# GpSimd copies of VectorE score tiles: one tile an instruction in place of two

## The chip, the cores and the metric

The kernel runs on one core of one Trainium2 chip. The metric is the device time of one launch in microseconds (us); for repeated runs it is the median. Besides these times there is one profiled execution, with a trace of every instruction, and it has a time of its own.

## The reference, cut to what matters

Two independent pieces are computed and set side by side in the output, (1, 2048, 1280) in bf16. Piece A is a state-space layer, of sequence 2048 and width 640. Piece B is an attention with 32 query heads of 20 dimensions that share one key head and one value head:

```python
q = (x @ wq).reshape(B, S, 32, 20).transpose(0, 2, 1, 3)
k, v = x @ wk, x @ wv
scores = jnp.einsum("bhqd,bkd->bhqk", q, k) * 20 ** -0.5
o = jnp.einsum("bhqk,bkd->bhqd", softmax(scores), v)
b = o.transpose(0, 2, 1, 3).reshape(B, S, 640) @ wo
a = 2 * (scan_over_time(x_A @ B_bar) @ C).real + x_A * D     # h = Lam_bar * h + Bu
return concatenate([a, b], -1)
```

Piece B needs 2048 x 2048 x 32 exponentials, which are most of the work of this kernel that is not a matmul.

## The kernel before, in words

**Tiles.** The scores are made in 2048 tiles of 128 keys by 512 queries of one head (`NTILE`, L403). Sixty-four tiles make a block: 16 groups of keys for 4 heads. There are 32 blocks, and the product of probabilities and values (PV) of one block is gathered in one PSUM bank (`pvbank`). A block's bank is evacuated (L1470) when all its tiles have been multiplied in, and then the next block's PV starts.

**Two ways to an exponential.** ScalarE (ACT) takes two or three score tiles in one `Exp` instruction (L1139) and writes bf16 probabilities to `PR`. Some tiles take the other way, called D tiles here. For a D tile VectorE (DVE) reads the scores from PSUM and writes them as 16-bit integers whose bits, read as bf16, are a coarse exponential (`fill_d`, L1316, instruction at L1329). Three copies follow, each with a constant added to the integers (`SHIFTS`, L419), and PV takes the tile and its three copies with differently scaled values (`VS`), so that a D tile has four buffers of `DR` and four PV matmuls. `DR` has 18 buffers (`NDS`). Through helpers, the trace shows the first step as `DR<-SC` or `DR<-MB` at L603, a copy by DVE as `DR<-DR` at L603, and a copy by GpSimd (POOL) as `DR<-DR,step` at L598.

**Who copies.** The list `d_open` holds the D tiles that still need copies, oldest first, each with the numbers of the shifts left (1, 2, 3 at first). Two functions make copies from it. `copy_source` (L1348) is DVE's: it copies two tiles in one instruction where it can, otherwise one. It acts when nine or more copies are outstanding (`BACKLOG`), or when the current block has all its tiles and only waits for them, and then with the high priority `CLOSE`. `pool_source` (L1378) is POOL's: it takes the oldest tile's next shift and the first two tiles that still need that shift; with fewer than two it returns nothing. Both call `copy` (L1392), which takes free buffers, builds the access patterns and enters the results for PV. POOL works on pairs of 16-bit values as 32-bit integers, and its addend `step` repeats the constant in both halves.

**The order of the work.** Nothing is ordered by the chip at run time. A planner (`Schedule`, L40) plays the program on five engines with a duration for each step, always picking the ready step of lowest priority number, and the order in which it started the steps on each engine is emitted as the program, with semaphore waits where one engine needs another's result (`Emitter`, L246). So a planned duration decides where steps stand, while the real one decides when they run. The planner's numbers near the change are 663 ns for a D tile's first step, 342 and 210 ns for a DVE copy of two and of one tile, and 1040 ns for a POOL copy of two (`POOL2`).

**The port.** Steps marked `port=True` share one resource between DVE and POOL in the plan (L134 to L139, L176 to L182): neither engine starts such a step while the other has one under way, DVE may not follow for another 60 ns after POOL's (`LOCK`), and POOL does not start one while DVE has a better one held back (`port_wanted`). POOL's emitted step also waits for DVE's last port step before it (`op.after`). The copies of both engines are port steps, and so are many steps of piece A on DVE: the products `u`, the scans `g`, the products of `g` with the tables, `W` and a few small ones.

**How many D tiles.** A D tile is started by `fill` (L1105), in place of the third tile of an ACT instruction or beside it, or alone by `d_source` (L1285). All of them ask for at least four free `DR` buffers, for piece A not to be behind its due times (`behind`, L1199), and for the share of D tiles to be below 0.25. Near the end of a block, `can_d` (L1261) asks for more buffers before it starts on the next block. Every tile that doesn't become a D tile goes to ACT.

Of the kernel before, what the change touches and what calls it, by code (L numbers as in the profile page):

```python
# [14 lines left out]
I32 = mybir.dt.int32  # L15
# [394 lines left out]
class Build:  # L410
# [967 lines left out]
    def pool_source(self):  # L1378

        s = self.s  # L1380
        can = [d for d in self.d_open if d[1].end is not None and s.seen(d[1], "pool") <= s.t]
        if not can or len(self.d_free()) < 2:
            return None
        k = can[0][2][0]
        two = [d for d in can if k in d[2]][:2]
        if len(two) < 2 or self.short(two):
            return None
        return Op("pool", [], self.POOL2, prio=1, port=True, hook=lambda op: self.copy(op, k, two, True))

    POOL2 = 1040.0  # L1390

    def copy(self, op, k, tiles, pool=False):  # L1392
        p = self
        src = [d[0].index for d in tiles]
        free = self.d_free()[:len(tiles)]
        dst = [h.index for h in free]

        def at(x):
            if len(x) == 1:
                return p.DR[:, x[0], :]  # L1400
            return bass.AP(tensor=p.DR, offset=512 * x[0], ap=[[512 * p.NDS, 128], [512 * (x[1] - x[0]), 2], [1, 512]])
        if pool:
            def words(x):
                return bass.AP(tensor=p.DR, offset=512 * x[0], ap=[[512 * p.NDS, 128], [512 * (x[1] - x[0]), 2], [1, 512]]).bitcast(I32)
            add = bass.AP(tensor=p.step, offset=k, ap=[[4, 128], [0, 2], [0, 256]])
            op.fns.append(self.tt(words(dst), words(src), add, ALU.add))
            op.reads.append("step")
        else:
            op.fns.append(self.ts(at(dst), at(src), float(self.SHIFTS[k][0]), 0.0, ALU.add, ALU.max))
        op.reads += [f"DR{i}" for i in src]  # L1410
        op.writes += [f"DR{i}" for i in dst]
        for d, h in zip(tiles, free):
            h.taken, h.left, h.users = True, 1, []
            d[0].left -= 1
            d[0].users.append(op)
            d[2].remove(k)
            _, _, _, b, kc, j = d
            self.d_left[b, j] -= 1
            self.pv_entry(b, kc, j, k, h, op)
        self.d_open = [d for d in self.d_open if d[2]]  # L1420
# [619 lines left out]
```

## Time and profile before

| what | us |
|---|---|
| median of 4 runs | 765.25 |
| the 4 runs | 764.29 to 766.17 |
| the profiled execution's own time | 769.72 |
| its span, first to last instruction | 767.9 |
| busy in the span: ACT | 739.5 |
| busy in the span: PE (matmuls) | 702.0 |
| busy in the span: DVE | 680.5 |
| busy in the span: POOL | 431.2 |

Counted in the trace: 461 D tiles (397 from the bank group `SC`, 64 from the bank `MB`), 402 POOL copies of two tiles each, 263 DVE copies of two tiles and 53 of one, and 667 `Exp` instructions. That is 402 x 2 + 263 x 2 + 53 = 1383 copies, three for each D tile, and 2048 - 461 = 1587 tiles for ACT (414 instructions of two, 253 of three).

A row of a profile group reads: line, engine, operation, what it writes and reads, how often, then busy us and mean ns of one, then the idle time of the engine just before it and what ended it. The span of an instruction overlaps its successor's by some tens of ns where they run back to back, so that count times mean is a little above the busy time.

### The profile page before, as it was taken

Reading aid. Unit: us, or ns where it says so; the run is one execution under the profiler, and the core shown is the slowest. Engines: PE = TensorE matmul, PEld = TensorE weight load, DVE = VectorE, ACT = ScalarE, POOL = GpSimd, SP = SyncE. Lnnn points to the kernel's source line nnn. Section 1 sums busy time; section 2 is a strip of 40 time slices with the busy share of each in tenths; the row PEclk is TensorE's granted clock in tenths of the full one; section 3 lists DMA queues with packets and bytes.
Section 4 is the critical chain, followed back from the end, with each engine's and each line's share of the span. In section 5 each row is a group of like instructions: output and inputs, shape, how many; then the busy total and the mean of one; then the engine's idle time right before and its main releaser. Section 6 shows DMA issues by size and latency. Waiting matters only on the chain.

```text
span 767.9 us, 24175 instructions
## 1 busy us (share of the span) xinstructions
PE 702.0 (91%) x10231; PEld 233.1 (30%) x10231; DVE 680.5 (89%) x1282; ACT 739.5 (96%) x693; POOL 431.2 (56%) x450
## 2 busy tenths in 40 slices
PE   9998898888899999998999999989999999989986
PEld 3322222222233223222332323223222232333323
DVE  6787899899999998999999898889999999987795
ACT  5799999999999999999999999999999999999994
POOL 3657655246756356744656657447664545557560
PEclk9699999999999999999999999999999999999999
DMA  9734121000000111110000111130000010000101
GB/s 195 116 96 81 43 59 50 18 8 11 8 17 26 30 35 32 49 46 18 16 15 10 37 32 39 32 68 17 11 14 12 18 31 21 24 11 25 31 6 43
DMA packets 61770, 27.87 MB, mean 36 GB/s; under 512 B 44936, under 2 KB 61664, under 8 KB 61664
## 3 DMA queue, kind: packets, MB, share of 16 engines
q1 hardware_dynamic: 60332, 26.20, 14.7%
q8 instruction: 81, 1.33, 0.7%
q10 hardware_dynamic: 1332, 0.13, 0.2%
q14 instruction: 25, 0.20, 0.1%
HBM read 8.31 MB, written 8.12 MB: 21 GB/s over the span
## 4 chain that ended last, share of the span: by engine, by line
ACT 78%; PE 17%; DMA 2%; DVE 1%; issue 1%; POOL 0%; ACTq 0%; SPq 0%; POOLq 0%; DVEq 0%
ACT PR L1139 77%; PE SC L588 5%; PE MB L584 5%; PE MB L588 5%; PE SC L584 1%; DMA wqf<-in_B_wq_dram 1%; DMA qd<-QP 1%; DMA xaT<-in_A_x_dram 0%; DVE DR L603 0%; ACT tab L1707 0%; ACT PR L1625 0%; POOL fr L603 0%; DVE fr L603 0%; DVE mab L818 0%; DVE prod L598 0%
## 5 line engine op out<-in xcount | busy, mean ns | idle before, releaser
L1139 ACT ACTIVATE PR<-SC 128x1024 bf16<-128x1024 f32 (+1 forms) x667 | 723.2, 1295 | 10.5 <-PE SC L588 8.3
L598 POOL TENSOR_TENSOR DR<-DR,step 128x512 int32<-128x512 int32 x402 | 410.3, 1046 | 306.1 <-DVE DR L603 124.6
L588 PE MATMUL SC<-QT,KT 32*128 32x512 bf16 x1984 | 262.6, 386 | 50.5 <-ACT PR L1139 42.4
L603 DVE TENSOR_SCALAR DR<-SC 128x512 int16<-128x512 f32 x397 | 265.1, 684 | 36.4 <-PE SC L588 25.8
L588 PE MATMUL MB<-DR,VS 128*32 128x512 bf16 x1844 | 231.8, 386 | 0.6 <-DVE pvsb L1470 0.3
L588 PE MATMUL MB<-PR,VP 128*32 128x512 bf16 x1587 | 213.7, 385 | 3.0 <-POOL DR L598 1.3
L588 PEld LDWEIGHTS SC<-QT,KT 32*128 32x128 bf16 x1984 | 67.8, 91 | 289.8 <-ACT PR L1139 194.3
L603 DVE TENSOR_SCALAR DR<-DR 128x1024 int16<-128x1024 int16 (+1 forms) x316 | 115.0, 418 | 12.5 <-PE MB L588 9.5
L588 PEld LDWEIGHTS MB<-DR,VS 128*32 128x32 bf16 x1844 | 57.9, 94 | 65.3 <-issue 36.5
L588 PEld LDWEIGHTS MB<-PR,VP 128*32 128x32 bf16 x1587 | 54.2, 94 | 62.6 <-issue 39.6
L584 PE MATMUL MB<-xaT,BT 128*32 128x512 bf16 x800 | 57.8, 382 | 1.9 <-DMA xaT<-in_A_x_dram 1.3
L598 DVE TENSOR_TENSOR prod<-MB,Z 128x1024 bf16<-128x1024 f32 x40 | 48.6, 1214 | 4.2 <-PE MB L584 3.8
L603 DVE TENSOR_SCALAR DR<-MB 128x512 int16<-128x512 f32 x64 | 43.5, 680 | 2.5 <-PE MB L588 2.3
L588 PE MATMUL MB<-KT,VZ 128*32 128x256 bf16 x840 | 45.0, 274 | 0.0
L1810 DVE TENSOR_TENSOR_SCAN g<-sc,hst,u 128x512 bf16<-128x512 f32 x30 | 41.2, 1373 | 0.0
L598 DVE TENSOR_TENSOR prod<-g,tab 128x1024 bf16<-128x1024 bf16 x40 | 34.1, 852 | 0.0
L584 PE MATMUL MB<-CT,xbT 128*32 128x512 bf16 (+1 forms) x640 | 29.7, 301 | 0.2 <-issue 0.2
L584 PE MATMUL MB<-CT,W 128*32 128x512 bf16 (+1 forms) x640 | 29.1, 301 | 0.8 <-DVE prod L598 0.5
L1627 DVE CAST stg<-MB 128x512 bf16<-128x512 f32 x35 | 23.8, 680 | 5.3 <-PE MB L584 5.2
L584 PE MATMUL MB<-WO,OP 128*32 128x128 bf16 (+1 forms) x560 | 25.5, 290 | 0.0
L584 PE MATMUL MB<-xbT,wqf 128*32 128x512 bf16 x340 | 25.2, 396 | 0.0
L588 PEld LDWEIGHTS MB<-KT,VZ 128*32 128x32 bf16 x840 | 21.3, 96 | 12.5 <-issue 5.9
(140 smaller groups left out, 370.7 us busy)
## 6 DMA issues: line engine op xcount, KB each, us to landing
out_dram<-stg SPq DMA_DIRECT2D x35, 128.0 KB, 1.9
qd<-QP SPq DMA_DIRECT2D x20, 128.0 KB, 1.8
QT<-qd SPq DMA_DIRECT2D x28, 80.0 KB
OP<-pvsb SPq DMA_DIRECT2D x108, 20.0 KB
rdP<-recs SPq DMA_DIRECT2D x108, 20.0 KB
CT<-in_B_x_dram SPq DMA_DIRECT2D x2, 640.0 KB, 5.6
WO<-in_B_wo_dram SPq DMA_DIRECT2D x1, 800.0 KB, 4.6
wqf<-in_B_wq_dram SPq DMA_DIRECT2D x1, 700.0 KB, 6.0
```

What stands on the lines that cost most here:

```text
L584: r = e.matmul(out[32 * j:32 * j + 32], lhsT=lhsT[:, 32 * j:32 * j + 32], rhs=rhs, start=start, stop=stop, tile_position=(0, 32 * j), skip ...
L588: return lambda e: e.matmul(out, lhsT=lhsT, rhs=rhs, start=start, stop=stop, **kw)
L598: return lambda e: e.tensor_tensor(out, a, b, op)
L603: return lambda e: e.tensor_scalar(out, a, s1, s2, op0=op0, op1=op1)
L1139: ex = self.act(lambda e: e.activation(dst, t[:, 0:512 * n], ACT.Exp, scale=1.0 / UNIT), 0.8333 * 512 * n + 64, table="exp", deps=[op], re ...
L1627: ev = self.dve(lambda e: e.tensor_copy(st, bank.ap), 620, deps=[prev], reads=[bank.key], writes=[key], prio=self.EV, gate=(lambda: last.e ...
L1810: o = self.dve(lambda e, ri=ri, init=init: e.tensor_tensor_scan(p.g[:, u, ri, :], rdec, p.u[:, ri, :], init, ALU.mult, ALU.add), 1280, por ...
```

## The change

POOL's copy takes one tile in place of two. `pool_source` keeps its first test (some tile open, two buffers free), takes the oldest tile alone, doesn't return empty-handed when there is no second one, and plans 600 ns for the step in place of 1040. The access patterns in `copy` get a length of one. DVE's copies and all the rules for D tiles are as before.

```diff
@@ pool_source
         if not can or len(self.d_free()) < 2:
             return None
         k = can[0][2][0]
-        two = [d for d in can if k in d[2]][:2]
-        if len(two) < 2 or self.short(two):
-            return None
-        return Op("pool", [], self.POOL2, prio=1, port=True, hook=lambda op: self.copy(op, k, two, True))
-
-    POOL2 = 1040.0
+        two = [d for d in can if k in d[2]][:1]
+        return Op("pool", [], 600.0, prio=1, port=True, hook=lambda op: self.copy(op, k, two, True))
+
@@ copy
         if pool:
             def words(x):
-                return bass.AP(tensor=p.DR, offset=512 * x[0], ap=[[512 * p.NDS, 128], [512 * (x[1] - x[0]), 2], [1, 512]]).bitcast(I32)
-            add = bass.AP(tensor=p.step, offset=k, ap=[[4, 128], [0, 2], [0, 256]])
+                return bass.AP(tensor=p.DR, offset=512 * x[0], ap=[[512 * p.NDS, 128], [512 * (x[-1] - x[0]), len(x)], [1, 512]]).bitcast(I32)
+            add = bass.AP(tensor=p.step, offset=k, ap=[[4, 128], [0, len(src)], [0, 256]])
```

## The prediction

> **What bounds the kernel now.** I read the busy shares first, then the chain that ended last, then the groups of instructions.
>
> ```profile
> PE 702.0 (91%) x10231; PEld 233.1 (30%) x10231; DVE 680.5 (89%) x1282; ACT 739.5 (96%) x693; POOL 431.2 (56%) x450
> ...
> ACT 78%; PE 17%; DMA 2%; DVE 1%; issue 1%; POOL 0%; ACTq 0%; SPq 0%; POOLq 0%; DVEq 0%
> ...
> L1139 ACT ACTIVATE PR<-SC 128x1024 bf16<-128x1024 f32 (+1 forms) x667 | 723.2, 1295 | 10.5 <-PE SC L588 8.3
> L598 POOL TENSOR_TENSOR DR<-DR,step 128x512 int32<-128x512 int32 x402 | 410.3, 1046 | 306.1 <-DVE DR L603 124.6
> ```
>
> The reader is to see that ACT's exponentials (L1139) fill the span, with 10.5 us of idle time before them, and that they hold most of the chain. POOL has no share of the chain. So the time is how many tiles ACT must take, and POOL bears on it only through the number of D tiles: ACT spends 723.2 / 1587 = 0.456 us on a tile, so each D tile more or less is worth 0.456 us. What limits the D tiles? The stages view (busy time of each engine in the part in which D tiles are made, from 40 to 748 us) shows how full the others are:
>
> ```profile
> core 0: us, PE busy (x) PEld busy (x) DVE busy (x) ACT busy (x) POOL busy (x), PEclk, DMA share, GB/s
> ...
> 40.00:748.00 708.00, 651.43 (x9428) 212.34 (x9428) 641.27 (x1160) 703.20 (x650) 408.18 (x400) 1.00 0.12 30
> ```
>
> DVE has 708.0 - 641.3 = 66.7 us free, and the view of its waits gives most of that to waits for a score matmul, the longest of which are about 1 to 2 us. POOL has 300 us free, but the waits of its copies say why it can't use them:
>
> ```profile
> POOL DR L598 <- DVE DR L603: 124.6, 33, 10.9
> POOL DR L598 <- DVE g L1810: 61.3, 16, 12.1
> POOL DR L598 <- PE MB L588: 37.1, 35, 6.5
> POOL DR L598 <- DVE u L598: 23.7, 6, 11.2
> ```
>
> They end with DVE steps, most of them port steps. I laid the starts and ends of POOL's instructions and of DVE's port steps (copies, u, g, prod from g, W and xbT, OP, the small ones) side by side, and counted outstanding copies at each moment as three for each first step ended less the copies started. Of 704 us from 44 to 748, POOL holds the port for 406, DVE alone for 210, and neither for 88. Of these 88 us, 25 have no copy outstanding and 28 have exactly three: one fresh tile, no second one to make a pair. So the port is 88% full, and nearly all the rest belongs to no copy that could be made, or to the rule of two. A block's change shows it (timeline of POOL, then of DVE):
>
> ```profile
> 394.46 1.04 POOL L598 TENSOR_TENSOR DR<-DR,step 128x512 int32<-128x512 int32 x1 [4.09 <-PE MB L588]
> 400.33 5.02 POOL L598 TENSOR_TENSOR DR<-DR,step 128x512 int32<-128x512 int32 x5 [4.83 <-PE MB L588]
> ```
>
> ```profile
> 395.41 2.31 DVE L603 TENSOR_SCALAR DR<-DR 128x1024 int16<-128x1024 int16 x7 [0.51 <-PE MB L588]
> 397.63 0.68 DVE L603 TENSOR_SCALAR DR<-SC 128x512 int16<-128x512 f32 x1
> 398.23 1.28 DVE L1810 TENSOR_TENSOR_SCAN g<-sc,hst,u 128x512 bf16<-128x512 f32 x1
> 399.42 0.67 DVE L603 TENSOR_SCALAR DR<-SC 128x512 int16<-128x512 f32 x1
> ```
>
> DVE clears the old block's copies, makes a first step at 397.6, scans, makes a second one at 399.4, and only after that POOL starts, at 400.3.
>
> **What the Trainium skill says.** The page "SBUF — State Buffer", section "Who interferes with whom", says that DVE and GpSimd share one pair of ports as an exclusive lock held for the whole instruction, against DVE steps in two-port modes or with two SBUF inputs. The trace agrees: a DVE copy has a median of 418 ns and a longest of 1258, as if it had stood behind a POOL copy. "Perfetto Trace Analysis", section "GPSIMD Engine Instruction", says to time GpSimd by start-to-start spacing rather than by the reported span; here five copies in a row took 5.02 us, 1.00 us each, against a reported 1.037, so the difference is small. "GPSIMD Engine Reference", section 3.1, gives 4497 ns for a tensor_tensor of 2048 fp32, which is 2.2 ns an element; by it I estimate 562 ns for 256 elements. The trace's pair, 1.00 us for 512, is 1.96 ns an element.
>
> **The change part by part.** *Price of a single.* The trace has no copy of one tile. From below: half a pair, 0.50 us, if an instruction had no fixed cost; nothing suggests a smaller one. From above: GpSimd's memsets took 204 ns for 128 columns and 101 ns for one, so some 0.1 us is fixed there, and its tensor_scalar VS of only 80 columns took 448 ns; with a fixed 0.4 us in the pair, a single is (1.00 - 0.4) / 2 + 0.4 = 0.70. I take 0.59, between the estimate above plus a little and the planner's 600 ns, which sets the order in any case.
>
> *What it adds on the port.* POOL makes 800 copies in this part: 800 x 0.59 = 472 us against 408, so 64 more. *What it removes.* POOL no longer waits for a second tile: 28 us of the port become usable. The sum is 36 us too much for the port, and DVE must take copies over from POOL. The forms of DVE's copies:
>
> ```profile
> L603 DVE TENSOR_SCALAR DR<-DR 128x1024 int16<-128x1024 int16 x263 | 104.0, 444 | 12.4 <-PE MB L588 9.5 <-POOL DR L598 2.1
> ...
> L603 DVE TENSOR_SCALAR DR<-DR 128x512 int16<-128x512 int16 x53 | 12.9, 286 | 0.1
> ```
>
> In pairs a copy costs DVE 0.444 / 2 = 0.222 us, so each copy that moves frees 0.59 - 0.22 = 0.37 us of the port: 36 / 0.37 = 97 copies move, and DVE has 97 x 0.222 = 21.5 us more. DVE's pairs aren't broken up, since the shifts are taken in order: what the oldest tile still needs, the next one needs too.
>
> *What follows for ACT.* If DVE were full, the 21.5 us would come out of D tiles. One D tile less frees 0.67 us of DVE (265.1 / 397) and three copies, 1.77 us of the port, which brings 1.77 / 0.37 = 4.8 copies back to POOL, 1.06 us of DVE: 1.73 us in all, so 21.5 / 1.73 = 12.4 tiles, or 5.7 us of ACT. DVE has 66.7 us free in short pieces, so a part is hidden; I put 70% on the path, since those pieces are times in which it has no tile to work on. That is 9 tiles and 4.0 us: 452 D tiles. Without any cover it is 5.7, and with full cover nothing.
>
> *What costs nothing here.* About 400 more POOL instructions come with their semaphore waits, most already met; PE, which waits for copies before PV, shows 1.3 us of waits on POOL in all, and may see up to 400 more waits where one used to cover two tiles. PE is busy 651 of 708 us and seldom holds ACT (8.3 us), which covers them; at 0.051 us for a wait instruction of PE in the trace they would be 20 us of PE if nothing covered them. No DMA is moved and no wait queue changes: POOL issues nothing else here, and behind a POOL copy stand only later copies.
>
> The sum: 769.7 + 4.0 = 773.7 us for a profiled execution. The profile ran 4.5 us above the median of the runs, so the forecast for the median is 765.25 + 4.0 = 769.2.
>
> **The rivals.** *Finer steps win (faster).* A DVE port step that finds POOL at work waits out what is left of a copy, on average half of 1.0 us now and half of 0.59 after. In 42 us of the trace both are on the port at once, which is such waiting; at 0.59 it would be 25, and 17 us of DVE come back. At each of 31 block changes the last copy also ends earlier, and a buffer that POOL fills is taken for 0.4 us less. If the single takes 0.53, the port pays 800 x 0.53 - 408 = 16 us and gets back 28: a gain of 12, or 12 / 0.31 = 39 copies and 8.6 us of DVE. A D tile then asks 0.67 + 3 x 0.53 / 0.31 x 0.222 = 1.81 us of DVE, so together that is 25.6 / 1.81 = 14 more D tiles, 6.4 us: 758.9. For it speak the 28 us and the long block changes; against it, that the plan counts 600 ns for the order, whatever the single takes. I leave the 17 us out of the forecast, since the 42 us also hold plain overlaps of ends and the 97 moved copies bring waits of their own; counted in full, they balance the toll where (800 p - 436) / (p - 0.222) x 0.222 = 17, at a single of p = 0.58, and below that this case decides.
>
> *Hidden (no change).* DVE's 66.7 us take the 97 copies in: 765.
>
> *The single is dear, or PE's waits show (much slower).* At 0.70 us, 0.1 above the plan, POOL runs late: 800 x 0.70 = 560, 152 more than before, 124 after the 28. Were all of it moved, that is 124 / 0.48 x 0.222 = 57 us of DVE, 70% of it on the path, at 0.67 + 2.1 / 0.48 x 0.222 = 1.64 us a tile: 24 tiles, 11 us: 776. POOL's waits in the trace let it catch up, which speaks against all of it.
>
> *The planner goes another way.* It picks greedily, and any new duration reshuffles the order; the D tiles may come out some tiles off the sum. I fold it into the width. That the change doesn't do what it says is not open: every POOL copy goes through the edited line.
>
> **How the numbers follow.** About 0.2% (1.5 us) is what a measurement of this kernel can tell from no change. The likeliest case, the port's toll, has 0.42 and lies between 766.5 and 773; finer steps 0.36, 753 to 763.5; hidden 0.10; dear 0.12, 773 to 785. Slower by over 0.2% is 0.41 + 0.12 = 0.53, within 0.2% is 0.01 + 0.10 = 0.11, faster 0.36. The range for 8 in 10 leaves out the far end of both: 756 to 779. The likeliest case's own range is 766.5 to 773.
>
> **What would show it.** About 452 D tiles instead of 461, with some 700 POOL copies near 0.59 us and more of DVE's; ACT's exponentials at 723.2 + 4 us; POOL's first copy after a block change right behind the first fresh tile. The prediction is wrong if the D tiles are as many or more, which would mean that latency or buffers and not port time limited them, or if ACT's idle time before L1139 grows well past 10.5 us, which would mean that the order, not the count, was hurt.

## The result, and the profile after

The kernel after takes 768.64 us (median; 764.16 to 776.18), the kernel before 765.75 in the runs beside it. The ratio is 1.003, 95% interval 1.0015 to 1.0045: slower by 0.3%, against 769.2 us predicted. The TensorE clock falls to half for stretches of 3.4 to 14 us at moments that differ from run to run, and the profile of before shown above had 14 us of it just where the exponentials begin; so the profile of before was taken once more (run `before_again` below), and its span of 761.3 us is what the 763.4 of after is compared with.

These stretches weigh on the medians too. In 15 of the 44 executions of after the mean granted clock was 0.993 or more, and their median is 765.46 us; the other 29 have 770.40. Of before, timed again beside the experiments, 100 of 158 executions had such a clock, with a median of 764.02, and the other 58 have 767.36 (for the runs of before beside this result the clock was not recorded). At a like clock, then, after is some 1.4 us (0.2%) slower than before; the rest of the 0.3% goes with more and longer stretches of half clock.

The page of after: busy shares, chain, exponentials, POOL's copies.

```profile
PE 699.0 (92%) x10198; PEld 232.9 (31%) x10198; DVE 689.4 (90%) x1354; ACT 737.6 (97%) x694; POOL 434.0 (57%) x739
...
ACT 77%; PE 18%; DVE 2%; DMA 1%; SPq 1%; issue 1%; POOL 1%; DVEq 0%; POOLq 0%
...
L1139 ACT ACTIVATE PR<-SC 128x1024 bf16<-128x1024 f32 (+1 forms) x668 | 721.3, 1289 | 7.5 <-PE SC L588 5.5
L598 POOL TENSOR_TENSOR DR<-DR,step 128x256 int32<-128x256 int32 x691 | 412.6, 629 | 299.9 <-DVE DR L603 131.9
...
L603 DVE TENSOR_SCALAR DR<-SC 128x512 int16<-128x512 f32 x405 | 269.4, 684 | 29.7 <-PE SC L588 23.3
```

The same two rows of before, profiled again (`before_again`):

```profile
L1139 ACT ACTIVATE PR<-SC 128x1024 bf16<-128x1024 f32 (+1 forms) x667 | 721.9, 1300 | 4.8 <-PE SC L588 3.1
L598 POOL TENSOR_TENSOR DR<-DR,step 128x512 int32<-128x512 int32 x402 | 410.8, 1048 | 298.1 <-DVE DR L603 123.9
```

The reader is to see three things. POOL is no busier than before: 691 copies in 413 us where it made 804 in 411. There are 405 D tiles from `SC`, with 61 from `MB` 466 in all, five more than before and not fewer. And ACT's idle time before L1139 went from 4.8 to 7.5 us. DVE's copies by form show where POOL's missing copies went:

```profile
L603 DVE TENSOR_SCALAR DR<-DR 128x1024 int16<-128x1024 int16 x324 | 123.4, 433 | 16.0 <-PE MB L588 12.0 <-POOL DR L598 3.1
...
L603 DVE TENSOR_SCALAR DR<-DR 128x512 int16<-128x512 int16 x59 | 15.2, 286 | 0.7 <-POOL DR L598 0.6
```

That is 324 x 2 + 59 = 707 copies against 579, 128 more. A block change of after (timeline of DVE, then of POOL) shows the earlier start. L1807 is the scan that stood at L1810 before:

```profile
394.08 0.68 DVE L603 TENSOR_SCALAR DR<-SC 128x512 int16<-128x512 f32 x1
394.68 1.27 DVE L1807 TENSOR_TENSOR_SCAN g<-sc,hst,u 128x512 bf16<-128x512 f32 x1
395.88 1.26 DVE L603 TENSOR_SCALAR DR<-SC 128x512 int16<-128x512 f32 x2
```

```profile
396.04 6.31 POOL L598 TENSOR_TENSOR DR<-DR,step 128x256 int32<-128x256 int32 x11 [9.33 <-DVE g L1807]
```

POOL starts as soon as the scan has left the port, while the second and third first steps still run. Counted as in the prediction, the time in which neither engine holds the port and just one fresh tile is open fell from 27.7 to 2.4 us. The time without any outstanding copy rose from 24.7 to 36.4, so about half of what was freed was put to use.

**Where the time went.** Back to back, an exponential of two tiles is followed by the next after 904 ns, one of three after 1331. Before has 414 and 253 of them: 414 x 0.904 + 253 x 1.331 = 711.0 us of work. After has 422 and 246: 708.9. From the first exponential's start to the last one's end it took 726.7 and 728.8 us. So ACT has 2.1 us less to do, and 19.9 us of stalls in place of 15.7. The spans differ by 2.1 us, as 4.2 - 2.1 says. Some 0.7 of the 4.2 us are due to a stretch of half clock at 647 us in the profile of after; 3.4 remain outside such stretches, which leaves 1.3 us, near the 1.4 of the executions at a like clock. Only a part of a stall shows as idle time, since ACT's reported spans overlap by 0.2 us where they run back to back.

### The profile page after: what moved, and what is told of

Same layout as the page of the kernel before. It is cut to its first block, busy times and chain, and to the rows that moved or that the text cites. A ratio compares the mean times of both kernels' runs of the same rounds, so it can differ in the third digit from the quotient of the medians.

```text
span 763.4 us, 24535 instructions
## 1 busy us (share of the span) xinstructions
PE 699.0 (92%) x10198; PEld 232.9 (31%) x10198; DVE 689.4 (90%) x1354; ACT 737.6 (97%) x694; POOL 434.0 (57%) x739
## 4 chain that ended last, share of the span: by engine, by line
ACT 77%; PE 18%; DVE 2%; DMA 1%; SPq 1%; issue 1%; POOL 1%; DVEq 0%; POOLq 0%
ACT PR L1139 76%; PE MB L588 6%; PE SC L588 5%; PE MB L584 5%; PE SC L584 1%; DVE DR L603 1%; DMA xaT<-in_A_x_dram 1%; DMA qd<-QP 0%; SPq L1516 0%; POOL DR L598 0%; ACT tab L1704 0%; DVE prod L598 0%; POOL fr L603 0%; DVE fr L603 0%; SPq L573 0%
## 5 line engine op out<-in xcount | busy, mean ns | idle before, releaser
L1139 ACT ACTIVATE PR<-SC 128x1024 bf16<-128x1024 f32 (+1 forms) x668 | 721.3, 1289 | 7.5 <-PE SC L588 5.5
L598 POOL TENSOR_TENSOR DR<-DR,step 128x256 int32<-128x256 int32 x691 | 412.6, 629 | 299.9 <-DVE DR L603 131.9
L603 DVE TENSOR_SCALAR DR<-SC 128x512 int16<-128x512 f32 x405 | 269.4, 684 | 29.7 <-PE SC L588 23.3
L588 PE MATMUL MB<-DR,VS 128*32 128x512 bf16 x1864 | 234.8, 385 | 2.6 <-DVE DR L603 1.4
L588 PE MATMUL MB<-PR,VP 128*32 128x512 bf16 x1582 | 227.2, 386 | 2.3 <-DVE pvsb L1467 0.9
L603 DVE TENSOR_SCALAR DR<-DR 128x1024 int16<-128x1024 int16 (+1 forms) x383 | 136.0, 410 | 16.7 <-PE MB L588 12.0
L588 PEld LDWEIGHTS MB<-PR,VP 128*32 128x32 bf16 x1582 | 57.2, 94 | 61.5 <-issue 38.3
L603 DVE TENSOR_SCALAR DR<-MB 128x512 int16<-128x512 f32 x61 | 41.3, 677 | 1.0 <-PE MB L588 0.7
L1807 DVE TENSOR_TENSOR_SCAN g<-sc,hst,u 128x512 bf16<-128x512 f32 x30 | 38.8, 1293 | 0.0
L598 DVE TENSOR_TENSOR prod<-g,tab 128x1024 bf16<-128x1024 bf16 x40 | 28.9, 721 | 0.0
L584 PEld LDWEIGHTS MB<-xaT,BT 128*32 128x32 bf16 x800 | 17.2, 95 | 24.5 <-issue 10.7
```

Of the source, the lines that this page charges most:

```text
L584: r = e.matmul(out[32 * j:32 * j + 32], lhsT=lhsT[:, 32 * j:32 * j + 32], rhs=rhs, start=start, stop=stop, tile_position=(0, 32 * j), skip ...
L588: return lambda e: e.matmul(out, lhsT=lhsT, rhs=rhs, start=start, stop=stop, **kw)
L598: return lambda e: e.tensor_tensor(out, a, b, op)
L603: return lambda e: e.tensor_scalar(out, a, s1, s2, op0=op0, op1=op1)
L1139: ex = self.act(lambda e: e.activation(dst, t[:, 0:512 * n], ACT.Exp, scale=1.0 / UNIT), 0.8333 * 512 * n + 64, table="exp", deps=[op], re ...
L1807: o = self.dve(lambda e, ri=ri, init=init: e.tensor_tensor_scan(p.g[:, u, ri, :], rdec, p.u[:, ri, :], init, ALU.mult, ALU.add), 1280, por ...
```

## The experiments

Twelve runs, each timed in five rounds beside the kernel before. The theory at first: the toll of the port is real, DVE paid it without losing D tiles, and the time is lost in execution, by results that come late. The rivals: POOL's or DVE's real time makes those stalls; or the order, which any change of a planned duration reshuffles, happens to be a little worse.

**before_again: no edit.**

> The kernel before, unchanged. Every theory expects a ratio of 1.000 within 0.2%. Its use is a profile: the first one of before had the granted clock lowered near 40 us, with 5.6 us of idle time of ACT around it. With the clock at full I expect a span of 760 to 763 us, ACT idle before L1139 of 3 to 6 us and the same 461 D tiles, 402 POOL copies and 316 DVE copies.

Ratio 0.9984 (0.9967 to 1.0002); span 761.3 us, idle time 4.8 us. It is the base line used above.

**split: the planner's order kept, the pairs cut.**

```diff
-            op.fns.append(self.tt(words(dst), words(src), add, ALU.add))
+            one = bass.AP(tensor=p.step, offset=k, ap=[[4, 128], [0, 256]])
+            for y, x in zip(dst, src):
+                op.fns.append(self.tt(p.DR[:, y, :].bitcast(I32), p.DR[:, x, :].bitcast(I32), one, ALU.add))
```

> The order and the plan of before (461 D tiles, pairs planned at 1040 ns), but each POOL copy of two tiles is emitted as two instructions of one tile. With the spacings seen, 570 ns for a single and 996 for a pair, POOL has 402 x 144 ns = 58 us more to do and nothing else moves. Theory price (POOL's longer copies delay PV and so ACT): 1.004 to 1.015. Theory plan (the price acts only through the planner, since POOL has 300 us of idle time): within 0.2% of 1.000.

Ratio 1.0268 (1.0234 to 1.0303), 21 us, more than either theory said. The waits of its PE and the row of its exponentials:

```profile
PE MB L588 <- POOL DR L598: 25.4, 55, 1.2
PE SC L588 <- ACT PR L1139: 21.4, 60, 1.0
...
```

```profile
L1139 ACT ACTIVATE PR<-SC 128x1024 bf16<-128x1024 f32 (+1 forms) x667 | 730.1, 1219 | 19.5 <-PE SC L588 13.3
L598 POOL TENSOR_TENSOR DR<-DR,step 128x256 int32<-128x256 int32 x804 | 496.9, 655 | 236.0 <-DVE DR L603 104.5
```

POOL still has 236 us of idle time, yet PE waits 25.4 us for it. In `before_again` that wait has no row at all. In a fixed order a PV matmul that waits for a late copy holds up the score matmuls queued behind it on PE, and so ACT. POOL's idle time is at other moments and doesn't help. DVE lost time as well: its waits for POOL's copies rose from 2.1 to 15.0 us and its busy time from 679.5 to 691.8. How the 21 us divide between the two ways isn't shown. So the price of singles is real where the plan doesn't know it: 58 us of POOL, by the spacings, cost 21 us. The idea that the price acts only through the planner fell here.

**single_on_pair: the price without the earlier start.**

```diff
-        two = [d for d in can if k in d[2]][:1]
+        two = [d for d in can if k in d[2]][:2]
+        if len(two) < 2 or self.short(two):
+            return None
+        two = two[:1]
```

> The kernel after, but POOL still waits for a second tile before it copies one: the price without the earlier start. The program then has 461 D tiles against 466 after and 461 before, with 643 copies on POOL and 740 on DVE. Theory plan with its two opposite parts: slower than after by 5 x 0.456 = 2.3 us or more, 1.005 to 1.012 against before, since DVE has 33 us more than before. Theory luck of the order: anything within 0.4% of before.

Ratio 1.0081 (1.0054 to 1.0108), 461 D tiles, as expected. With as many D tiles and as much work for ACT as before (711.1 us), it is 6.2 us slower, so what it loses is stalls; after, with the earlier start, is at 1.003.

**pair_or_single: the earlier start without the price.**

```diff
-        two = [d for d in can if k in d[2]][:1]
-        return Op("pool", [], 600.0, ...)
+        two = [d for d in can if k in d[2]][:2]
+        if self.short(two):
+            two = two[:1]
+        return Op("pool", [], 600.0 if len(two) == 1 else 1040.0, ...)
```

> POOL copies two tiles where there are two and one where there is one: the earlier start without the price. The program has 471 D tiles, 858 copies on POOL and 555 on DVE (24 fewer than before). Theory plan: 10 D tiles are 4.6 us of ACT, so 0.993 to 0.997. Theory luck of the order: within 0.4% of before, either way.

Ratio 0.9999 (0.9971 to 1.0027). The 471 D tiles are there and ACT's work is 4.2 us less, but the gain is not: the stalls, counted as above, rose from 15.7 to 21.2 us, of which 2 us lie in stretches of half clock after the start. The expected 0.993 to 0.997 lies just outside the interval. D tiles alone don't make time.

**Copies cut short, to take POOL's and DVE's real time away.** The order stays. In two runs POOL's access patterns get 256 columns instead of 512, in two those of DVE's copies. Since PV would read what nothing wrote, `DR` is zeroed once at the start; `after_init` has that zeroing alone.

```diff
+        self.zero_op.fns.insert(0, lambda e: e.memset(self.DR[:], 0))
...
-                return bass.AP(tensor=p.DR, offset=512 * x[0], ap=[..., len(x)], [1, 512]]).bitcast(I32)
+                return bass.AP(tensor=p.DR, offset=512 * x[0], ap=[..., len(x)], [1, 256]]).bitcast(I32)
```

> The kernel after, its order unchanged, but each POOL copy covers 256 of the 512 columns; the rest of the copy is left out (DR is zeroed once at the start). A single should then be spaced by some 330 ns instead of 570, 691 x 0.24 = 166 us less on POOL. Against a full-clock profile of before (span 761.3) the kernel after (763.4) has 2.1 us less of exponentials by ACT and 4.2 us more of stalls. Theory POOL (its real time makes those stalls): 3 us or more faster than after, 0.999 or less against before. Theory order (the stalls come from the order on PE and from DVE): within 1.5 us of after, 1.001 to 1.005.

> The same cut in the kernel before: pairs of 2 x 256 columns, spaced by some 550 ns instead of 996, 180 us less on POOL, order unchanged. Theory POOL: faster, but by less than the kernel after gains, since before has fewer stalls (15.7 against 19.9 us): 0.997 to 0.999. Theory order: 0.999 to 1.001.

> The kernel after, its order unchanged, but each of DVE's copies covers 256 of the 512 columns (the rest is left out). A pair should be spaced by about 200 ns instead of 336: 324 x 134 ns = 43 us less on DVE. Theory DVE (its 128 copies more than before make first steps late, and so score matmuls and ACT): 3 us or more faster than after, 0.999 or less against before, and at least 2 us more gained than in the kernel before. Theory order: a gain equal to that of before within 1 us.

> The same cut in the kernel before: 263 x 134 ns = 35 us less on DVE, order unchanged. Theory DVE: a gain of 1 to 2 us, 0.997 to 0.999. Theory order: 0.998 to 1.000, the same gain as in the kernel after.

> The kernel after with nothing left out, and only the zeroing of DR at the start that the runs with short copies carry. It is their base line. In the profiles that zeroing moved the first exponential from 23.2 to between 27.4 and 28.7 us. So this should run 4 to 5.5 us slower than after: 1.009 against before. Theory POOL: the run with POOL's copies cut short (1.0062) is then 2 us or more faster than this. Theory order: the two are within 1 us.

| run | ratio to before | interval |
|---|---|---|
| after_init | 1.0098 | 1.0062 to 1.0134 |
| after_poolshort | 1.0062 | 1.0042 to 1.0082 |
| after_dveshort | 1.0059 | 1.0042 to 1.0077 |
| before_poolshort | 1.0064 | 1.0043 to 1.0086 |
| before_dveshort | 1.0036 | 1.0024 to 1.0048 |

The first four expectations had left out what the zeroing costs: DVE's memset takes 3.9 us, and the first exponential starts 4.3 to 5.5 us late. Against their base line the two cuts in after are worth 0.36 and 0.39%, 2.8 and 3.0 us, with intervals that overlap. But five of the six executions of `after_init` had a mean clock below 0.993, against 8 of 22 with POOL's copies cut and 11 of 22 with DVE's. At 0.993 or more they took 769.2 us (one execution), 769.1 and 768.2, and in the three profiles the stalls outside stretches of half clock sum to 15.7, 15.6 and 14.4 us. At a like clock, then, the cut on POOL is worth next to nothing, and that on DVE some 1 us.

Before has no base line of its own; with 4.3 to 5.5 us for the late start (1.0056 to 1.0072) its cut on POOL gains nothing or little and its cut on DVE 1.5 to 2.8 us, and all 22 executions of the latter had the higher clock, where before beside it had it in 37 of 66. So neither theory of an engine's real time finds support: 691 x (570 - 355) ns = 149 us less on POOL, or about 40 us less on DVE, give the kernel after some 1 us at most, by these few executions. A POOL that is late against the plan cost 21 us in `split`; one that is early brings almost nothing.

**plan595 and plan605: the change itself, in other orders.**

```diff
-        return Op("pool", [], 600.0, prio=1, ...
+        return Op("pool", [], 595.0, prio=1, ...    # and 605.0
```

> The kernel after with 595 ns planned for a single instead of 600: the same design in another order, with 471 D tiles against 466. By the spacings of back-to-back exponentials its ACT work is 706.9 us, 4.1 less than before and 2.0 less than after. Theory stalls grow with D tiles: the gain is eaten again, 1.000 to 1.004. Theory toll (singles cost a fixed 4.2 us of stalls): 1.000. Theory D tiles alone: 0.995. Theory luck of the order: anywhere from 0.995 to 1.006.

> As the last, with 605 ns: 464 D tiles, ACT work 709.8 us, 1.2 less than before. Theory stalls grow with D tiles: 1.001 to 1.002. Theory toll: 1.004. Theory D tiles alone: 0.998. Theory luck of the order: anywhere from 0.995 to 1.006, and not in line with the run at 595.

Ratios 1.0022 (1.0005 to 1.004) at 595 and 0.9993 (0.9972 to 1.0014) at 605. The same design at 605, in an order that 5 ns of planned time reshuffled, is not slower than before. At a mean clock of 0.993 or more the medians are 766.04 us at 595, 765.46 at 600 and 764.26 at 605, against 764.02 of before. A fixed toll of singles (1.000 and 1.004) is refuted at 605; D tiles alone (0.995) at 595.

**pair1000: pairs, planned near their real spacing.**

```diff
-    POOL2 = 1040.0
+    POOL2 = 1000.0
```

> The kernel before with POOL2 at 1000 ns, near the 997 that its pairs took, instead of 1040: pairs only, 468 D tiles, ACT work 708.0 us, 3.0 less than before. Theory toll (only singles bring stalls): 0.996. Theory stalls grow with D tiles: 1.000 to 1.002. Theory luck of the order: either.

Ratio 1.0047 (1.0028 to 1.0067): no singles at all, seven D tiles more, and slower than before. The toll theory's 0.996 is refuted again. The theory of stalls that grow with D tiles had said 1.002 at most, and the ratio misses that too. But 21 of the 22 executions had a mean clock below 0.993 (17 of 51 of before, 3 of 14 of plan605 in the same rounds). The one execution above that, at 0.996, took 765.71 us, 1.002 times the 764.01 of before at such a clock. So it isn't shown that at a like clock this order is slower than the change. What half clock does is seen in its profile, where it holds for 6.8 of the 8 us of this window (busy us of PE, weight loads, DVE, ACT and POOL; 0.57 is the mean clock):

```profile
402.00:410.00 8.00, 8.00 (x74) 1.64 (x70) 5.25 (x9) 6.10 (x7) 6.21 (x7) 0.57 0.11 31
```

PE is busy all the time and ACT idles for 1.9 us. Where these stretches come is not chance alone. The fourteen profiles hold ten that begin between 50 and 740 us, and in each of the ten PE had been busy for only 38 to 70% of the 3.4 us just before, where 93 to 96% is the median of such pieces. In three of the four profiles with the order of after one begins at the same point of the work, near 650 us. So an order can bring lulls of PE, and with them a lower clock, though not every lull did.

The stages view from 60 to 740 us, for before_again, plan605, after, pair1000 and plan595 in this order (busy us of PE, weight loads, DVE, ACT and POOL, then the clock):

```profile
60.00:740.00 680.00, 626.46 (x9134) 204.79 (x9138) 619.91 (x1120) 678.00 (x627) 391.30 (x384) 1.00 0.11 28
```

```profile
60.00:740.00 680.00, 631.29 (x9185) 206.36 (x9181) 623.00 (x1170) 677.03 (x627) 395.89 (x670) 1.00 0.11 28
```

```profile
60.00:740.00 680.00, 626.54 (x9091) 205.07 (x9088) 625.37 (x1183) 675.37 (x626) 388.79 (x652) 1.00 0.11 28
```

```profile
60.00:740.00 680.00, 629.43 (x9112) 202.47 (x9108) 620.41 (x1100) 674.85 (x622) 407.51 (x399) 0.99 0.11 28
```

```profile
60.00:740.00 680.00, 632.19 (x9214) 206.89 (x9210) 630.26 (x1185) 674.21 (x627) 399.64 (x680) 1.00 0.11 28
```

The fourth number is ACT. Its free time is 2.0, 3.0, 4.6, 5.2 and 5.8 us, at 461, 464, 466, 468 and 471 D tiles. It grows with the D tiles in these five, whether POOL copies singly or in pairs. But two of the five hold stretches of half clock in this window, of 3.4 us in after and 6.8 in pair1000; without the 0.5 and 1.9 us that ACT was free there, after has 4.1 and pair1000 3.3, and the row is no longer in order. What would have been gained in work is given back as waiting, in good part at least. It is not the whole rule: `single_on_pair` has 6.7 us free at 461 D tiles, 1.9 of them in such a stretch, and `pair_or_single` 4.6 at 471. These are single profiles, and a difference of 0.5 us between two of them says little.

**What one such stall looks like.** In the timeline of after, the largest of the later ones:

```profile
521.78 0.40 PE L584 MATMUL MB<-xaT,BT 128*32 128x512 bf16 x4 [1.95 <-DMA xaT<-in_A_x_dram]
522.11 0.10 PEld L588 LDWEIGHTS SC<-QT,KT 32*128 32x128 bf16 x3 [0.23 <-issue]
...
522.55 3.40 ACT L1139 ACTIVATE PR<-SC 128x1536 bf16<-128x1536 f32 x3 [1.04 <-PE SC L588]
```

PE stands at a matmul of piece A until a transposed load has landed; the score matmuls behind it in the order come late, and ACT idles for 1.04 us. Nothing in it is a POOL copy. The load itself was issued late (queue of SP; after, then `before_again`):

```profile
515.15 1.26 SPq L573 DMA_TRANSPOSE xaT<-in_A_x_dram  x1
516.45 0.59 SPq L1500 DMA_DIRECT2D dn<-sums  x1
517.09 1.26 SPq L573 DMA_TRANSPOSE xaT<-in_A_x_dram  x1
```

```profile
503.32 2.95 SPq L573 DMA_TRANSPOSE xaT<-in_A_x_dram  x2
```

In before the last two of the five loads went out together from 503.3 us. In after they stand behind eleven other transfers in the queue and went out at 515.2 and 517.1. The new plan had reordered the queue; the prediction's "No DMA is moved" did not hold.

## Why the prediction was right in the number and wrong in the way

**Right: the time, the sign, the parts on the port.** The single takes 0.570 us from start to start, against 0.59 assumed. POOL made 691 copies in all, against some 700. The rule of two did cost the 28 us of the port, and they came free, though 12 us more passed with no copy to make. DVE took over 128 copies, against 97, and its copies took 138.6 us against 116.9, 21.7 more where 21.5 were forecast.

**Wrong: the step from DVE to ACT.** The prediction put 70% of DVE's 21.5 us on the path, as nine lost D tiles: 452. There are 466, and as many or more was its own sign of being wrong. In the stage from 40 to 748 us DVE's busy time rose only from 643.9 us (`before_again`) to 650.2, well within the 64 us that it had free. Its other steps on the port had become shorter (`before_again`, then after):

```profile
L598 DVE TENSOR_TENSOR prod<-g,tab 128x1024 bf16<-128x1024 bf16 x40 | 34.0, 850 | 0.0
```

```profile
L598 DVE TENSOR_TENSOR prod<-g,tab 128x1024 bf16<-128x1024 bf16 x40 | 28.9, 721 | 0.0
```

The spans of all that DVE does besides copies and first steps sum to 311.8 us in `before_again` and 299.8 in after; the other profiles agree, with 299.3 to 302.0 for `single_on_pair`, plan595 and plan605, and 316.5 for pair1000. That is the 17 us of "finer steps", which the prediction had left out of its sum: 12 of them came. In the plan, moreover, the price alone took no D tile (461 in `single_on_pair`), and the earlier start alone brought ten (471 in `pair_or_single`). So of the rivals "hidden" and "finer steps" had the better account of DVE.

**Wrong: a D tile is worth 0.456 us.** The work of ACT does fall, by 2.1 us for five tiles (0.42 each, since most of them replace the third tile of an instruction). But four kernels with 466 to 471 D tiles ran at 0.9999 to 1.0047 times before, and none of them is faster than before at a like clock. In the prediction's own terms the costs that it found covered were the ones that counted: it found PE's and POOL's waits covered because they were short in the profile of before, and `split` shows that 58 us more on POOL, under 300 us of idle time, cost 21 us. In the change itself, where the plan knew the longer copies, this is seen only in part: PE's weight loads waited 18.3 us for POOL's copies, against 7.8 before, and which waits made the 3.4 us of new stalls isn't shown.

**Of the 0.3%, what is the change's own.** The price alone (`single_on_pair` against before) is 0.81%, 6.2 us; the earlier start gives back 0.5%. They look like the two opposite parts of the prediction, 64 and 28 us of the port, and by its conversion, 70% of 64 / 0.37 x 0.222 / 1.73 x 0.456, the first would be 7.1 us and the second 3.1. But the agreement is of sizes only. The lost D tiles through which it was reckoned did not occur, `pair_or_single`, which has the earlier start without the price, gained nothing, and 5 ns in the planner's number move the same design from 1.003 to 0.9993. The sign of this small result is that of one order among several. The number was met by luck: at a like clock the change costs some 1.4 us, against 4.0 forecast, and stretches of half clock, for which the prediction has no term, made up the rest of the 2.9 measured. What makes one order stall 3 or 4 us more than another stays open: the stalls are some 60 small ones, and no cut of one engine's work removed them.

## What to carry to other kernels

When a planner writes the order of all engines, a change of one step's planned duration is a new order everywhere: repeat the design with neighbouring durations before believing a gain or a loss of a few tenths of a per cent, and compare executions that were granted a like clock. Idle time of an engine in such a program is no reserve: its results are due at fixed places in other queues, and lateness there is paid by whatever stands behind. Being earlier than the plan brought little here. Work that is moved off the bounding engine counts only with the stalls that the move brings; measure the bounding engine's work and its stalls apart.

## What the runs showed of the hardware

GpSimd's 32-bit addition follows a straight line: 355 ns from start to start for 128 elements a partition (`after_poolshort`), 570 for 256, 997 for 512. That is a fixed 143 ns or so and 1.67 ns an element, so that a pair saves 143 ns over two singles. The reported span is 41 or 42 ns above the spacing at each length (397, 612 and 1037 or 1039). The prediction's estimate of 562 ns from a rate at 2048 elements was near 570 only because a rate above the one measured here stood in for the fixed part.

An exponential by ScalarE is spaced by 904 ns for 1024 columns and 1331 for 1536, that is 427 ns for each 512 columns and 50 fixed. The stretches of half TensorE clock during the work lasted 3.41, 6.83, 10.24 or 13.65 us in all these profiles, whole multiples of the shortest.
